# A list scheduler's price for SyncE transfers and its rank for the preparation of later chunk pairs

## The chip, the cores and the metric

One core of one Trainium2 chip. The metric is the device time of one execution in microseconds (us), lowest is best; three runs of the kernel before gave 1113.38, 1113.78 and 1109.34 us, median 1113.38 us.

## The reference

Input: r, k, v, w, a, b of shape (4 batches, 8 heads, 768 steps, 40). Each of the 32 heads runs a linear recurrence over 768 steps with a 40x40 state:

```
y_t   = r_t @ state
Sa    = state @ a_t
state = state * w_t - outer(Sa, b_t) + outer(v_t, k_t)
```

The outputs y of all heads form 3072 tokens of 320 features. They pass a first layer, `max(x@w1, x@w2, x@w3) @ w_out` with 768 hidden units, and a second, `((x@w_a) * (x@w_b)) @ w_out` with 1536 hidden units. All is float32; the matmuls of the two layers are split into a rounded high part and a low part, so that each product takes several matmuls.

## The kernel before, in words

The recurrence is cut into 24 chunks of 32 steps, taken as 12 pairs. `prep(p)` makes what pair p needs and depends on the inputs alone; `chain(c)` carries the state through chunk c; `gather(p)` turns the result of a pair into a 320x256 tile `xf`; `moe_a(p)` is the first layer for that pair's 256 tokens; `moe_b(n)`, n = 0 to 5, is the second layer for 512 tokens each and starts when the recurrence has ended.

**The preparation.** It loads decay and key tiles, runs two scans per chunk on VectorE (L394, L398), and forms products on GpSimd or VectorE and TensorE (L427, L445). A 32x32 triangular system for each head and chunk is then moved through scratch tensors in HBM, since its rows have to change partitions: `BD` is stored at L459 and read back as `BU` at L465; `solve` forms the inverse with alternating multiplies (L499 on GpSimd, L500 on VectorE) and reductions (L501, into `TXp`, then `TW` and `TC`); the inverse is stored to `TD` (L471) and read back as `TT` (L475); the correction block is stored to `ED` (L480) and read back as `NB` (L483).

**The chain.** In each chunk `zmm` (L616) needs the state and the products of the preparation; `half` (L630) needs `TT`; `umm` (L643) needs `NB`; `smm` (L663) gives the new state, which the next chunk's L616 needs. Around them stand transposes (L576, L592, L689) and the output products (L701, L719). `gather` stores at L732 and reads `xf` back at L737 and L739.

**The first layer.** Its weights come in 24 pieces (L759), which VectorE unpacks with four instructions each (L749 to L752); L827 and L852 to L856 are its matmuls, 144 and 48 per pair. `stage_b` unpacks the second layer's weights in 24 more pieces in the same way (load at L916, stores to the scratch tensor `WD` at L923 and L924), and `weights_b` reads them back (L930 to L934) when the recurrence's buffers are free.

**What sets the order.** No order is written by hand. Every operation is recorded with an engine, an estimated duration, a latency after its end, its dependences and a rank `pri`; the function `run` of the class Plan then places one operation after another, each engine taking the ready operation with the earliest start, and among those within 0.05 of it the lowest rank. The latency enters twice: an operation's users count as ready that much later, and the rank is lowered by BL = 0.04 times the length of the longest path behind the operation:

```
            t = d + l + o["pre"]
            bl[i] = t + max((bl[j] for j in out[i]), default=0.0)
            o["pri"] = o["pri"] - BL * bl[i]
```

Ranks that matter here: the chain has 0.001 c (its side products up to 0.5 more), gather 0.2, the first layer's work outside TensorE 0.6 and its matmuls 2 + p, the first layer's weights 3, the second layer's weights 5. The function `dma` records every transfer of SyncE; transfers that ScalarE issues have a function of their own (`adma`) with a latency of 2.0 + bytes/200e3. Where TensorE would idle in the plan, `run` puts matmuls of an identity matrix (L275) into the gap. The program holds the order that results, engine by engine; a transfer that waits holds up all transfers behind it on SyncE's queue.

Of the kernel before, what the change touches and what calls it, by code (L numbers as in the profile page):

```python
# [27 lines left out]
DMIN = 0.4  # L28
# [19 lines left out]
class Plan:  # L48
# [8 lines left out]
    def op(self, eng, dur, fn, r=(), w=(), ps=(), fin=(), pri=0.0, lat=None, after=(), pre=0.0, cls=0, alt=(), act=1.0, bias=None):  # L57

        i = len(self.ops)
        deps = set(after)  # L60
        for k in r:
            if k in self.lw:
                deps.add(self.lw[k])
        for k in w:
            if k in self.lw:
                deps.add(self.lw[k])
            deps.update(self.rd.get(k, ()))
        for k in r:
            self.rd.setdefault(k, []).append(i)
        for k in w:  # L70
            self.lw[k] = i
            self.rd[k] = []
        deps.discard(i)
        ways = {eng: (dur, fn, 0.0)}
        ways.update({e: (d, f, bias if bias is not None else 0.0 if pri < BIASP else BIAS) for e, d, f in alt})
        self.ops.append(dict(i=i, ways=ways, bias=bias, deps=deps, ps=tuple(ps), fin=tuple(fin), pri=pri, lat=lat, pre=pre, cls=cls, act=act))
        return i
# [159 lines left out]
def body(nc, tc, ia, out_ap):  # L237
    from contextlib import ExitStack

    V, A, G, T, SP = nc.vector, nc.scalar, nc.gpsimd, nc.tensor, nc.sync  # L240
    es = ExitStack()
    P = Plan(8)
    op = P.op
    npair = NP

    def dv(n, ps=False):
        return 0.15 + n * 0.00105 if ps else 0.12 + n * 0.0014
# [5 lines left out]
        return 0.4 + n * 0.0023  # L253

    def dma(fn, nbytes, r=(), w=(), pri=0.0, pre=1.2):
        return op("SP", max(DMIN, nbytes / 300e3), fn, r=r, w=w, pri=pri, lat=1.0, pre=pre)

    def adma(fn, nbytes, r=(), w=(), pri=0.0, after=()):

# [70 lines left out]
    def setup():  # L330
        def zero(t, keys, eng, v=0.0, pri=-5.0):
            n = int(np.prod(t.shape[1:]))
            E = {"DVE": V, "POOL": G}[eng]
            op(eng, 0.06 + n * (0.00105 if eng == "DVE" else 0.0009), lambda w_: E.memset(t, v), w=keys, pri=pri)

        R2 = range(2)
        dma(lambda w_: SP.dma_start(con, ia["con"]), 98e3, w=["con"], pri=-9)
        dma(lambda w_: SP.dma_start(TC.rearrange("p i j -> p (i j)")[:, 0:32], ia["one"]), 16e3, w=["TC"], pri=-3)
        zero(d1, ["d1"], "DVE")
        zero(gd, ["gd"], "DVE")  # L340
        zero(RB, [("RB", g) for g in R2], "POOL", pri=-4.5)
        for i, b in enumerate(bank):
            op("ACT", ac(512), lambda w_, b=b: A.activation(b, RB[:, 0].rearrange("p u t -> p (u t)"), AF.Copy), r=[("RB", 0)], w=["bank"], pri=-5.0)
        zero(ZR[0], [(k, 0, g) for k in ("ZRs", "ZRv") for g in R2], "POOL", pri=-4.2)
        zero(YL, [(k, x) for k in ("YLg", "YLr") for x in R2], "POOL", pri=-4)
        zero(YR[0], [(k, 0, x, h) for k in ("YRy", "YRs", "YRs2") for x in R2 for h in R2], "POOL", pri=-4)
        zero(ST, ["ST", ("STx", 0), ("STx", 1)], "POOL", pri=-3)
        for i in range(2):
            op("ACT", ac(512), lambda w_, i=i: A.activation(
                NB[i].rearrange("p c h t -> p (c h) t"), TC.rearrange("p i j -> p (i j)")[:, 0:32].unsqueeze(1).to_broadcast([128, 16, 32]), AF.Copy), r=["TC"], w=[("NB", i, j) for j in range(4)], pri=-3)  # L350
        dma(lambda w_: SP.dma_start(TXp, ia["eye"]), 270e3, w=["TX"], pri=-0.55)


    def prep(p):
        b, kb_ = p % NPB, p % 2
        pr = 1.0 + p - 1.5
        P_, K_, Z_ = Pp[b], KT[kb_], ZL[b]
        parts = [(0, 1), (1, 2)] if p < NSPL else [(0, 2)]

# [23 lines left out]
        for cc in range(2):  # L383
# [8 lines left out]
            else:  # L392
# [8 lines left out]
               r=[("R", cc, 0), ("R", cc, 1), "d1"], w=rc, pri=pr)  # L401
# [4 lines left out]
            for src, k, n in ((Rp[:, cc, :, 0:32], rc, 1), (P_[:, cc, :, 1:33], pc, 0)):  # L406
                op("ACT", 0.61, lambda w_, cc=cc, src=src, n=n: A.activation(
                    Rp[:, cc, :, 0:32], src, AF.Square, accum_out=gd[:, 4 * p + 2 * cc + n:4 * p + 2 * cc + n + 1]),
                   r=k, w=rc + ["gd"], pri=pr + 0.5)
            for g in range(2):  # L410
# [3 lines left out]
                   r=pc, w=[("Za", b, g, cc)], pri=pr, alt=[("DVE", dv(512), lambda w_, cc=cc, g=g, r0=r0: V.tensor_tensor(  # L414
                       Z_[r0:r0 + 64, cc, g], Z_[r0:r0 + 64, cc, g], P_[r0:r0 + 64, cc, :, 0:32], ALU.mult))])
            pn = ("a", "kb", p, cc)
            za = [("Za", b, g, cc) for g in range(2)]
            if p >= KG:
# [12 lines left out]
                for n in range(4):  # L431
# [5 lines left out]
                       r=[pn, "con"], w=[("Zk", b, g, cc)], fin=[pn] if n == 3 else (), pri=pr)  # L437
# [12 lines left out]
            for g in range(2 if p < KG else 0):  # L450
# [4 lines left out]
                   r=[pn, "con"], w=[("Zk", b, g, cc)], fin=[pn] if g else (), pri=pr)  # L455
# [7 lines left out]
        for h in range(2):  # L463
            n, f0 = (512, 0) if h == 0 else (496, 528)
            dma(lambda w_, h=h, n=n, f0=f0: SP.dma_start(  # L465
                BU[64 * h:64 * h + 64].rearrange("p i j -> p (i j)")[:, 0:n],
                BD[b].rearrange("u s t -> u (s t)")[:, f0:f0 + n]), 131e3, r=bk, w=[("BU", h)] + ([("BB", 0)] if h else []), pri=pr)
        solve(p)
        for h in range(2):
            q = 16 * (1 - h)  # L470
# [15 lines left out]
                16e3, r=[("ED", b, h) for h in range(2)], w=[("NB", p % 2, j)], pri=pr)  # L486

    def solve(p):
        pr = 1.0 + p - 1.5
        cnt = [0]  # L490

        def mm(out_v, tmpshape, a, bb, rk, wk):
            i = cnt[0] % 2
            cnt[0] += 1
            n = int(np.prod(tmpshape))
            names = "abcd"[:len(tmpshape)]
            kw = {k: v for k, v in zip(names[1:], tmpshape[1:])}
            tv = TP[i][:, 0:n].rearrange("p (" + " ".join(names) + ") -> p " + " ".join(names), **kw)
            op("POOL", 0.35 + n * 0.0026, lambda w_: G.tensor_tensor(tv, a, bb, ALU.mult), r=rk, w=[("TP", i)], pri=pr,  # L499
               alt=[("DVE", dv(n), lambda w_: V.tensor_tensor(tv, a, bb, ALU.mult))])  # L500
            op("DVE", dv(n, True), lambda w_: V.tensor_reduce(out_v, tv, AX.X, ALU.add), r=[("TP", i)], w=wk, pri=pr)  # L501

        def diag(tile, off, blk, cnt_, rows, cols, rs=32, cs=1):
            base = tile[:, 0:1, 0:1]
            a = base.copy() if False else base
            return bass.AP(tensor=a.tensor, offset=a.offset + off, ap=[list(a.ap[0]), [blk, cnt_], [rs, rows], [cs, cols]])

        bu = [("BU", 0), ("BU", 1)]
        for t in range(1, 8):
            a = diag(TX, 0, 264, 2, t, t)  # L510
            u = diag(BU, t, 264, 2, 1, t, 0, 32)
            u = bass.AP(tensor=u.tensor, offset=u.offset, ap=[list(u.ap[0]), [264, 2], [0, t], [32, t]])
            o = diag(TX, t, 264, 2, t, 1)
            o = bass.AP(tensor=o.tensor, offset=o.offset, ap=[list(o.ap[0]), [264, 2], [32, t]])
            mm(o, (2, t, t), a, u, bu + ["TX"], ["TX"])

        def prod(dst, d_off, d_rs, L, l_off, l_rs, R, r_off, r_rs, nr, nt, nj, rk, wk):
            tl = 512 // (nt * nj)
            for c0 in range(0, nr, tl):
                k = min(tl, nr - c0)  # L520
                lb, rb, db = L[:, 0:1, 0:1], R[:, 0:1, 0:1], dst[:, 0:1, 0:1]
                a = bass.AP(tensor=lb.tensor, offset=lb.offset + l_off + c0 * l_rs, ap=[list(lb.ap[0]), [l_rs, k], [0, nt], [1, nj]])
                u = bass.AP(tensor=rb.tensor, offset=rb.offset + r_off, ap=[list(rb.ap[0]), [0, k], [1, nt], [r_rs, nj]])
                o = bass.AP(tensor=db.tensor, offset=db.offset + d_off + c0 * d_rs, ap=[list(db.ap[0]), [d_rs, k], [1, nt]])
                mm(o, (k, nt, nj), a, u, rk, wk)


        prod(TW, 0, 8, TX, 0, 32, BU, 8, 32, 8, 8, 8, bu + ["TX"], ["TW"])
        prod(TX, 8, 32, TW, 0, 8, TX, 264, 32, 8, 8, 8, ["TX", "TW"], ["TX"])

        op("ACT", 0.3, lambda w_: A.activation(BU[64:128, 0:8, 16:32], BU[0:64, 8:16, 16:32], AF.Copy), r=bu, w=[("BB", 0)], pri=pr)
        for h in range(2):
            op("ACT", 0.35, lambda w_, h=h: A.activation(TU[64 * h:64 * h + 64], TX[64:128, :, 0:16], AF.Copy), r=["TX"], w=[("TU", h)], pri=pr)
        k = bu + [("BB", 0), ("TU", 0), ("TU", 1)]
        prod(TC, 0, 16, BU, 16, 32, TU, 0, 16, 8, 8, 8, k, ["TC"])
        prod(TC, 8, 16, BU, 16, 32, TU, 8, 16, 8, 8, 16, k, ["TC"])
# [477 lines left out]
    stage_b()  # L1014
    ma.extend(range(a0, len(P.ops)))
    prep(0)
    if npair > 1:
        prep(1)
    for p in range(npair):
        a0 = len(P.ops)  # L1020
        chain(2 * p)
        chain(2 * p + 1)
        if p + 2 < npair:
            prep(p + 2)
        gather(p)
        att.extend(range(a0, len(P.ops)))
        a0 = len(P.ops)
        moe_a(p)
        ma.extend(range(a0, len(P.ops)))
# [218 lines left out]
```

## Time and profile before

| | |
|---|---|
| runs | 1113.38 us median of 3 (1109.34 to 1113.78) |
| profiled execution | 1115.33 us, of which the span of instructions is 1113.5 us |
| busy: TensorE, VectorE, ScalarE, GpSimd | 1054.6, 641.5, 481.0, 253.6 us |
| chain that ended last | TensorE 68%, DMA 12%, VectorE 11%, issue 3% |
| moved | 128.99 MB, most of it before 760 us |

The span has two halves that differ. Up to about 713 us the recurrence and the first layer run side by side on all engines; from there the second layer alone keeps TensorE busy. Busy time of TensorE is the union of pipelined matmuls, so it says where nothing at all ran, not how dense the rest was.

### The profile page before, as it was taken

How to read it: one execution, taken by the hardware profiler on the slowest of the kernel's cores; microseconds unless marked ns; L12 is line 12 of the kernel's file. 1: busy time of each engine (PE TensorE's matmuls, PEld its weight loads, DVE VectorE, ACT ScalarE, POOL GpSimd, SP SyncE). 2: the span in 40 equal slices, each digit the busy share in tenths (PEclk: the TensorE clock that was granted, in tenths of full speed). 3: DMA queues.
4: the chain of work that ended last, by engine and by line, in shares of the span. 5: the costliest groups of instructions: out<-in, count | busy, mean ns of one | idle time of the engine just before them, and what ended most of it. 6: DMA issues, size and time to landing. Idle time of an engine off the chain costs nothing.

```text
span 1113.5 us, 34271 instructions
## 1 busy us (share of the span) xinstructions
PE 1054.6 (95%) x14826; PEld 949.6 (85%) x14826; DVE 641.5 (58%) x1052; ACT 481.0 (43%) x1112; POOL 253.6 (23%) x219
## 2 busy tenths in 40 slices
PE   8899898989799999989999999999999999999997
PEld 7777798889798888888888889988888888888886
DVE  6778598768797966887787744333223232322222
ACT  5246364737465554647363662222223222322221
POOL 3343264324244542424242310000000000000000
PEclk8989798989899988999999999999999999999999
DMA  8746764666567657585846556870101000000000
GB/s 254 178 93 170 176 158 100 148 155 175 134 189 164 173 139 175 131 195 140 202 104 158 148 154 186 250 174 11 43 1 53 1 24 1 1 24 1 24 1 26
DMA packets 177661, 128.99 MB, mean 116 GB/s; under 512 B 122848, under 2 KB 150624, under 8 KB 176544
## 3 DMA queue, kind: packets, MB, share of 16 engines
q1 hardware_dynamic: 174048, 120.84, 42.8%
q10 hardware_dynamic: 3456, 5.90, 1.5%
q8 instruction: 118, 1.93, 0.7%
q14 instruction: 39, 0.32, 0.1%
HBM read 96.02 MB, written 30.67 MB: 114 GB/s over the span
## 4 chain that ended last, share of the span: by engine, by line
PE 68%; DMA 12%; DVE 11%; issue 3%; SPq 2%; ACT 2%; POOL 1%; ACTq 0%; DVEq 0%; POOLq 0%
PE bank L967 24%; PE bank L827 11%; PE bank L975 4%; PE bank L977 4%; PE bank L976 4%; DMA wraw<-in_wpa_dram 2%; DMA WD<-wraw 2%; PE bank L719 2%; PE bank L663 2%; PE bank L275 2%; PE bank L701 2%; PE bank L630 2%; PE bank L576 1%; DMA ED<-TC 1%; PE bank L852 1%
## 5 line engine op out<-in xcount | busy, mean ns | idle before, releaser
L985 DVE TENSOR_TENSOR bas<-bank,bas 128x512 f32<-128x512 f32 x72 | 49.8, 692 | 213.5 <-PE bank L967 207.1
L967 PE MATMUL bank<-bxhi,bw 128*128 128x512 f32 x576 | 156.3, 393 | 0.0
L967 PEld LDWEIGHTS bank<-bxhi,bw 128*128 128x128 f32 x576 | 106.1, 188 | 20.8
L987 ACT ACTIVATE bgh<-bas 128x512 fp32r<-128x512 f32 x72 | 45.6, 633 | 143.9 <-DVE bas L985 142.0
L984 ACT ACTIVATE bas<-bank 128x512 f32<-128x512 f32 x72 | 43.0, 598 | 137.3 <-PE bank L967 137.3
L827 PE MATMUL bank<-xhi,whi 128*128 128x256 f32 x432 | 99.0, 312 | 0.0
L827 PE MATMUL bank<-xhi,wlo 128*128 128x256 f32 x432 | 91.3, 295 | 0.0
L827 PE MATMUL bank<-xlo,whi 128*128 128x256 f32 x432 | 90.9, 294 | 0.0
L967 PE MATMUL bank<-bxlo,bw 128*128 128x512 f32 x288 | 89.7, 393 | 0.0
L975 PE MATMUL bank<-bo,bgh 128*128 128x320 f32 x288 | 88.9, 309 | 0.0
L977 PE MATMUL bank<-bo,bgl 128*128 128x320 f32 x288 | 88.8, 308 | 0.0
L976 PE MATMUL bank<-bo,bgh 128*128 128x320 f32 x288 | 88.8, 308 | 0.0
L988 DVE TENSOR_TENSOR bgl<-bas,bgh 128x512 fp32r<-128x512 f32 x72 | 49.8, 692 | 47.0 <-ACT bgh L987 46.9
L842 DVE TENSOR_TENSOR hm<-bank,hm 128x512 f32<-128x512 f32 x72 | 49.6, 689 | 46.8 <-PE bank L827 45.6
L827 PEld LDWEIGHTS bank<-xhi,whi 128*128 128x128 f32 x432 | 70.7, 203 | 2.9
L827 PEld LDWEIGHTS bank<-xhi,wlo 128*128 128x128 f32 x432 | 71.8, 204 | 0.1
L827 PEld LDWEIGHTS bank<-xlo,whi 128*128 128x128 f32 x432 | 71.4, 203 | 0.0
L499 POOL TENSOR_TENSOR TP<-TXp,BU 128x50 f32<-128x50 f32 (+7 forms) x67 | 47.5, 709 | 101.6 <-DVE TXp L501 56.5
L412 POOL TENSOR_TENSOR ZL<-ZL,Pp 64x512 f32<-64x512 f32 x37 | 54.9, 1484 | 57.3 <-DVE Pp L394 29.7
L275 PE MATMUL bank<-con 128*128 128x128 f32 x452 | 62.7, 297 | 2.8 <-DMA con<-in_con_dram 2.8
L967 PEld LDWEIGHTS bank<-bxlo,bw 128*128 128x128 f32 x288 | 54.1, 188 | 12.3
L827 PE MATMUL bank<-xl,wt 128*128 128x256 f32 x216 | 63.3, 293 | 0.5 <-POOL xl L819 0.5
(161 smaller groups left out, 2496.8 us busy)
## 6 DMA issues: line engine op xcount, KB each, us to landing
wraw<-in_wpb_dram SPq DMA_DIRECT2D x24, 480.0 KB
KT<-in_kb_dram SPq DMA_DIRECT2D x20, 384.0 KB
bw<-WD SPq DMA_DIRECT2D x12, 512.0 KB
WD<-wraw ACTq DMA_DIRECT2D x24, 240.0 KB
WD<-wca SPq DMA_DIRECT2D x24, 240.0 KB
Pp<-in_wf_dram SPq DMA_DIRECT2D x10, 528.0 KB
Rp<-in_wr_dram SPq DMA_DIRECT2D x10, 528.0 KB
wraw<-in_wpa_dram SPq DMA_DIRECT2D x12, 384.0 KB
```

Source lines behind the costliest of these rows:

```text
L275: P.keep = lambda b: T.matmul(bank[b][:, 0:128], ident, ident, start=True, stop=True)
L412: op("POOL", po(512), lambda w_, cc=cc, g=g, r0=r0: G.tensor_tensor(Z_[r0:r0 + 64, cc, g], Z_[r0:r0 + 64, cc, g], P_[r0:r0 + 64, cc, :, 0: ...
L499: op("POOL", 0.35 + n * 0.0026, lambda w_: G.tensor_tensor(tv, a, bb, ALU.mult), r=rk, w=[("TP", i)], pri=pr, alt=[("DVE", dv(n), lambda w ...
L827: T.matmul(ps, w, x, start=(i == 0), stop=(i == 7))
L842: op("DVE", dv(512, True), lambda w_, pn=pn: V.tensor_tensor(f(hm), bank[w_[pn]], f(hm), ALU.max), r=[pn], w=["hm"], fin=[pn], pri=ep)
L967: T.matmul(ps, w, x, start=(k == 0), stop=(k == 7))
L975: T.matmul(o, gh[:, c], oh, start=ff == 0, stop=False)
L976: T.matmul(o, gh[:, c], ol, start=False, stop=False)
L977: T.matmul(o, gl[:, c], oh, start=False, stop=ff == 11)
L985: op("DVE", dv(512, True), lambda w_, j=j, pb=pb: V.tensor_tensor(tb["as", j], bank[w_[pb]], tb["as", j], ALU.mult), r=[pb], w=[("bas", j) ...
L987: op("ACT", ac(512), lambda w_, j=j, k=k: A.activation(tb["gh", k], tb["as", j], AF.Copy), r=[("bas", j)], w=[("gh", k)], pri=ep)
L988: op("DVE", dv(512), lambda w_, j=j, k=k: V.tensor_tensor(tb["gl", k], tb["as", j], tb["gh", k], ALU.subtract), r=[("bas", j), ("gh", k)], ...
```

## The change

The latency that the scheduler books for a SyncE transfer was 1.0 us for any size and becomes 2.0 us plus bytes/200e3, the same form as for ScalarE's transfers (for 131,000 bytes 2.66 instead of 1.0). The rank of `prep(p)` and `solve(p)` was p - 0.5 and becomes 0.6 p - 0.5: pair 0 stays at -0.5, pair 2 goes from 1.5 to 0.7, pair 6 from 5.5 to 3.1, pair 11 from 10.5 to 6.1. No operation of the computation is added or removed.

```
--- before.py
+++ after.py
@@ -253,7 +253,7 @@
         return 0.4 + n * 0.0023
 
     def dma(fn, nbytes, r=(), w=(), pri=0.0, pre=1.2):
-        return op("SP", max(DMIN, nbytes / 300e3), fn, r=r, w=w, pri=pri, lat=1.0, pre=pre)
+        return op("SP", max(DMIN, nbytes / 300e3), fn, r=r, w=w, pri=pri, lat=2.0 + nbytes / 200e3, pre=pre)
 
     def adma(fn, nbytes, r=(), w=(), pri=0.0, after=()):
 
@@ -353,7 +353,7 @@
 
     def prep(p):
         b, kb_ = p % NPB, p % 2
-        pr = 1.0 + p - 1.5
+        pr = -0.5 + 0.6 * p
         P_, K_, Z_ = Pp[b], KT[kb_], ZL[b]
         parts = [(0, 1), (1, 2)] if p < NSPL else [(0, 2)]
 
@@ -486,7 +486,7 @@
                 16e3, r=[("ED", b, h) for h in range(2)], w=[("NB", p % 2, j)], pri=pr)
 
     def solve(p):
-        pr = 1.0 + p - 1.5
+        pr = -0.5 + 0.6 * p
         cnt = [0]
 
         def mm(out_v, tmpshape, a, bb, rk, wk):
```

The order that comes out differs on every engine. Three places follow.

SyncE, around the tables of pair 4, before the change. `XD`, `xf` belong to the gather of pair 3; `TD`, `TT`, `ED`, `NB` to the tables of pair 4; `BD`, `BU` to pair 5:

```order
L732 DMA XD_81<-XY 40x4x256 x2
L374 DMA Pp_120<-in_wf_dram 128x1056
L862 DMA X2D_84<-x2s 128x512
L737 DMA xf<-XD_81 128x2x256
L739 DMA xf<-XD_81 64x256 x2
L863 DMA X2D_84<-x2s 64x256
L916 DMA wraw<-in_wpb_dram 128x960
L471 DMA TD_75<-TXp 64x512 x2
L459 DMA BD_73<-ZL_128 32x16x32 x4
L374 DMA Rp<-in_wr_dram 128x1056
L480 DMA ED_78<-TC 64x128 x2
L475 DMA TT_140<-TD_75 32x16x32 x4
```

and the stretch that holds the same tables of pair 4 after the change:

```order
L471 DMA TD_75<-TXp 64x512 x2
L556 DMA XX<-in_vx_dram 32x640
L924 DMA WD<-wca 128x480
L916 DMA wraw<-in_wpb_dram 128x960
L556 DMA XX<-in_vx_dram 32x640
L475 DMA TT_140<-TD_75 32x16x32
L567 DMA YL<-in_ry_dram 40x512 x2
L475 DMA TT_140<-TD_75 32x16x32 x3
L556 DMA ZR_136<-in_vz_dram 32x640 x2
L480 DMA ED_78<-TC 64x128 x2
L459 DMA BD_73<-ZL_128 32x16x32 x2
L563 DMA XT<-in_vt_dram 80x16x32
```

The tables' stores no longer stand behind the read-back of the gather (L737, L739); they now come before that gather's own store. Other transfers stand between L471 and L475 in both.

TensorE, up to the `half` (L630) of the first chunk of pair 4, before:

```order
L856 MATMUL bank_65<-hlo,woh 128x256
L827 MATMUL bank_67<-xhi,whi 128x256 x2
L827 MATMUL bank_67<-xhi,wlo 128x256 x2
L827 MATMUL bank_67<-xlo,whi 128x256 x2
L827 MATMUL bank_67<-xt_109,wt_103 128x256
L827 MATMUL bank_67<-xl_110,wt_103 128x256
L827 MATMUL bank_66<-xhi,whi 128x256 x2
L827 MATMUL bank_66<-xhi,wlo 128x256 x2
L827 MATMUL bank_66<-xlo,whi 128x256 x2
L827 MATMUL bank_66<-xt_109,wt_103 128x256
L827 MATMUL bank_66<-xl_110,wt_103 128x256
L630 MATMUL bank_64<-Zs,TT_140 32x40 x32
```

and after:

```order
L827 MATMUL bank_68<-xhi,wlo 128x256 x2
L827 MATMUL bank_68<-xlo,whi 128x256 x2
L827 MATMUL bank_68<-xt_109,wt_103 128x256
L827 MATMUL bank_68<-xl_110,wt_103 128x256
L701 MATMUL bank_69<-RB,XT 64x64 x16
L576 MATMUL bank_65<-con,KT_124 128x104 x4
L827 MATMUL bank_64<-xhi,whi 128x256 x2
L827 MATMUL bank_64<-xhi,wlo 128x256 x2
L827 MATMUL bank_64<-xlo,whi 128x256 x2
L827 MATMUL bank_64<-xt_109,wt_103 128x256
L827 MATMUL bank_64<-xl_110,wt_103 128x256
L630 MATMUL bank_70<-Zs,TT_140 32x40 x32
```

Before the change 99 rows stand between this chunk's L616 and its L630, with 112 matmuls of L827 and 24 of L852 to L856; after it 13 rows with 16 matmuls of L827.

SyncE near the end of the recurrence, after the change (`bw`, `bt`, `bo` are the second layer's weights, read back; `wraw` is the load of a piece of them that is still to be unpacked):

```order
L932 DMA bt_10352<-WD 64x2x128 x2
L934 DMA bo_10353<-WD 128x2x320
L862 DMA X2D_94<-x2s 128x512
L863 DMA X2D_94<-x2s 64x256
L932 DMA bt_10352<-WD 64x2x128 x2
L934 DMA bo_10353<-WD 128x2x320 x2
L941 DMA xr_10354<-X2D_87 128x8x64
L916 DMA wraw<-in_wpb_dram 128x960
L924 DMA WD<-wca 128x480
L944 DMA xr_10354<-X2D_87 64x4x64 x2
L941 DMA xr_10354<-X2D_88 128x8x64
L924 DMA WD<-wca 128x480
```

Before the change the 24th and last load of L916 stands ahead of all reads of `bw`; now it stands behind the reads of the first nine parts.

Over the whole program the identity matmuls of L275 rise from 226 to 256 instructions (the trace shows two records for each).

## Rows read from the trace of the kernel before

**Rows 1.** Busy time by stretch: length, PE, PEld, DVE, ACT, POOL, granted clock, DMA.

```profile
0.00:150.00 150.00, 135.33 (x2289) 114.78 (x2290) 109.09 (x194) 72.00 (x190) 55.87 (x54) 0.87 0.67 168
150.00:650.00 500.00, 462.13 (x9643) 429.57 (x9645) 388.60 (x638) 284.06 (x704) 192.75 (x161) 0.94 0.62 156
650.00:713.00 63.00, 62.78 (x875) 60.57 (x870) 28.53 (x49) 21.22 (x47) 4.96 (x4) 1.00 0.71 210
713.00:1113.50 400.50, 394.31 (x2033) 344.63 (x2031) 115.32 (x173) 103.69 (x174) 0.00 (x0) 1.00 0.11 31
```

**Rows 2.** Timeline of TensorE: L616 of chunks 6, 7 and 8.

```profile
208.15 0.80 PE L616 MATMUL bank<-ZR,ZL 128*32 128x40 f32 x64
...
247.54 0.80 PE L616 MATMUL bank<-ZR,ZL 128*32 128x40 f32 x64
...
261.08 0.71 PE L616 MATMUL bank<-ZR,ZL 128*32 128x40 f32 x55
```

**Rows 3.** Waits of TensorE: us in total, times, longest.

```profile
PE bank L630 <- DMA TT<-TD: 19.9, 15, 3.1
...
PE bank L643 <- DMA NB<-ED: 3.5, 6, 1.2
```

**Rows 4.** Timeline of TensorE, L630 of chunk 8; in brackets the idle time before it.

```profile
284.51 0.97 PE L630 MATMUL bank<-Zs,TT 32*32 32x40 f32 x6 [1.90 <-DMA TT<-TD]
```

**Rows 5.** Timeline of VectorE, the last reduction into pair 4's inverse.

```profile
267.50 0.69 DVE L501 TENSOR_REDUCE TXp<-TP 128x64 f32<-128x512 f32 x1
```

**Rows 6.** Timeline of SyncE's queue around the tables of pair 4.

```profile
267.68 1.18 SPq L862 DMA_DIRECT2D X2D<-x2s  x1
272.05 0.37 SPq L737 DMA_DIRECT2D xf<-XD  x1
272.51 1.13 SPq L739 DMA_DIRECT2D xf<-XD  x2
...
274.95 2.27 SPq L471 DMA_DIRECT2D TD<-TXp  x2
...
281.45 4.66 SPq L475 DMA_DIRECT2D TT<-TD  x4
```

**Rows 7.** Waits of SyncE's queue for a store to land before its read-back.

```profile
SPq L483 <- DMA ED<-TC: 13.3, 6, 4.1
...
SPq L737 <- DMA XD<-XY: 8.0, 7, 2.6
...
SPq L475 <- DMA TD<-TXp: 7.1, 3, 2.9
...
SPq L465 <- DMA BD<-ZL: 5.4, 4, 1.6
```

**Rows 8.** Groups by line: busy us, mean ns of one, idle before.

```profile
L275 PE MATMUL bank<-con 128*128 128x128 f32 x452 | 62.7, 297 | 2.8 <-DMA con<-in_con_dram 2.8
...
L752 DVE SCALAR_TENSOR_TENSOR wraw<-wraw,wca 128x480 f32<-128x480 uint32 (+3 forms) x48 | 32.5, 677 | 0.4
L750 DVE SCALAR_TENSOR_TENSOR wraw<-wraw,wca 128x480 uint32<-128x480 uint32 (+3 forms) x48 | 30.6, 637 | 0.4
...
L749 DVE TENSOR_SCALAR wca<-wraw 128x480 uint32<-128x480 uint32 (+3 forms) x48 | 26.2, 546 | 44.7 <-DMA wraw<-in_wpa_dram 23.6 <-DMA wraw<-in_wpb_dram 10.4 <-DMA WD<-wca 6.1
...
L751 DVE TENSOR_SCALAR wca<-wraw 128x480 uint32<-128x480 uint32 (+3 forms) x48 | 22.4, 466 | 0.3
```

**Rows 9.** Chain that ended last: start us, us, what; a block of 16 first-layer matmuls.

```profile
660.78 2.10 PE bank L827 x16
```

**Rows 10.** Timeline of SyncE's queue: the last piece of weights, loaded and stored.

```profile
662.67 0.39 SPq L916 DMA_DIRECT2D wraw<-in_wpb_dram  x1
...
679.58 0.54 SPq L924 DMA_DIRECT2D WD<-wca  x1
...
721.73 0.78 SPq L930 DMA_DIRECT2D bw<-WD  x1
...
732.09 0.60 SPq L934 DMA_DIRECT2D bo<-WD  x1
```

More of the change, by code (lines that the diff above doesn't have):

```diff
@@ L255, in dma @@
     def dma(fn, nbytes, r=(), w=(), pri=0.0, pre=1.2):
-        return op("SP", max(DMIN, nbytes / 300e3), fn, r=r, w=w, pri=pri, lat=1.0, pre=pre)
+        return op("SP", max(DMIN, nbytes / 300e3), fn, r=r, w=w, pri=pri, lat=2.0 + nbytes / 200e3, pre=pre)
     def adma(fn, nbytes, r=(), w=(), pri=0.0, after=()):
@@ L355, in prep @@
         b, kb_ = p % NPB, p % 2
-        pr = 1.0 + p - 1.5
+        pr = -0.5 + 0.6 * p
         P_, K_, Z_ = Pp[b], KT[kb_], ZL[b]
@@ L488, in solve @@
     def solve(p):
-        pr = 1.0 + p - 1.5
+        pr = -0.5 + 0.6 * p
         cnt = [0]
```

## The prediction

> **What bounds the kernel now.** I read the busy time by stretch first [rows 1]. [...]
>
> [...] The state products (L616) of chunks 6, 7 and 8 begin at 208.2, 247.5 and 261.1 us [rows 2]: from the first chunk of a pair to its second 39 us pass, from the second to the next pair only 14. The two chunks do the same work, so the first one waits for something: the waits of TensorE name it [rows 3], the tables TT (19.9 us in 15 waits) and NB (3.5 us in 6), together 23.4 us. For pair 4 the trace shows the whole way. The last reduction into the inverse ends at 268.2 us [rows 5], but its store to TD starts only at 274.95 and the read-backs into TT only at 281.45 [rows 6]; L630 then starts at 284.5 after an idle 1.9 us [rows 4]. Ahead of the store SyncE's queue held the gather's read-back (L737, L739), which waited for its own store to land. Such waits, a store just ahead of its read-back, cost that queue 13.3 + 8.0 + 7.1 + 5.4 = 33.8 us [rows 7]. A plan that books 1.0 us for each of these transfers puts the read-back too close behind the store, and everything behind it stands.
>
> **The change, part by part.**
>
> *Room between stores and read-backs.* I counted, in the two orders, the transfers that stand on SyncE between the last store and the first read-back, over all 12 pairs: for BD and BU 30 before and 83 after, for XD and xf 40 and 70, for ED and NB 41 and 61, for TD and TT 51 and 55. In all 162 become 269. The 33.8 us of queue time should shrink. On TensorE this is worth at most the 23.4 us of [rows 3], and nothing at least, if the tables are late for another reason (the solve itself). I take half, -12 us: three of the four gaps grow by half or more, but the one that ends in TT, which is the larger wait, hardly grows, and its gain has to come from the places where the store itself stands earlier, as in pair 4.
>
> *Preparation ahead of the first layer's weights.* Ahead of the last reduction for pair 2 stand 231 VectorE instructions before and 200 after; the largest part is six weight pieces less, counted at L749, and five less at L750 to L752. By [rows 8] that is 6 x 0.55 + 5 x (0.64 + 0.47 + 0.68) = 12 us of VectorE time in front of pair 2's tables. What is gained there is lent: when pair 2's L630 comes up in TensorE's order, 16 matmuls of L827 are behind it instead of 80. A block of 16 takes 2.10 us [rows 9], 0.131 each, so 64 matmuls are 8.4 us that have to be done later on an engine that is 92% busy. The identity matmuls ahead of that L630 also fall, from 205 to 194. Between a gain of 12 and a loss of 8.4 I take 0.
>
> *Identity matmuls.* 30 more instructions are 60 more records; one record costs 62.7/452 = 0.139 us [rows 8], so 8.3 us if all of them take time from real work and 0 if all stand in real gaps. 13 of the 30 stand behind the last L616, where TensorE is busy for 62.8 of 63 us today [rows 1]; the others fall mostly where TensorE waits anyway. I take 13 x 2 x 0.139 = +3.6 us.
>
> *The last piece of second-layer weights* now loads behind the reads of nine finished parts. Today the last piece takes 17 us from its load at 662.7 to its last store at 679.6, and the read of the remaining three parts runs from 721.7 to 732.1 [rows 10], 10 us. So 27 us after the second layer's start the three parts can be there; 72 blocks in 400.5 us [rows 1] are 5.6 us each, so the tenth block, the first to need them, comes after 50 us. I cost it at 0; the cover is nine blocks that have their weights. If it went, the rest of those 27 us would show as a hole around 760 us; I leave 5 us for it in the range.
>
> Sum against the profiled execution, 1115.3 us: -12 + 0 + 3.6 + 0 = -8.4, so 1106.9. That execution lies 1.95 us above the median of the runs, and the same -8.4 from 1113.4 gives **1105.0 us**.
>
> **The rivals.** About 0.5%, 5.6 us here, is what a measurement of this kernel can tell from no change.
>
> *Full order (no change).* TensorE is 92% busy between 150 and 650 us, and both orders hold the same real work. If the waits of [rows 3] only change place, because what comes early in one pair is paid for in the next, the time stays at 1113, within 5.6. For it: everything lent in the early stage comes back before the last chunk (1440 matmuls of L827 stand ahead of the last L616 in both orders). Against it: a wait for the queue's head is work for nobody, and its cause is reduced.
>
> *The preparation sets the pace.* If VectorE's order decides when a pair starts, both gains arrive in full: 12 us early and 23.4 in the waits, less the 8.3 of identity matmuls, -27 and so 1086. For it: 39 against 14 us in [rows 2]. Against it: TensorE has too little idle time to give so much.
>
> *Halves without cover (slower).* Between L616 and L630 of the first chunk, the new order has little for TensorE to do in three pairs: 16 first-layer matmuls instead of 136 in pair 4, 24 instead of 96 in pair 6, 8 instead of 80 in pair 7. The plan trusts that the tables are there by then. If they come no earlier than today, the lost cover is 264 matmuls, 264 x 0.131 = 35 us of standing still; it decides as soon as TT lands later than that little work ends, in pair 4 some 2 us of first-layer matmuls and a few transposes after L616. Part of it would be caught up, as the deferred matmuls fill later gaps: those are 38 us wide in all, of which some 15 could take it. So +35 - 15 + 3.6 = +24, 1137. For it: in pair 4 three of the four read-backs of TT now stand behind a transfer (L567) that must wait for a product of the chain. Against it: the store of TD comes before the gather there.
>
> [...]
>
> That the change does not do what it says is excluded: the orders differ on every engine as shown.
>
> **How the numbers follow.** The forecast, -5.6 to -20 us, has a chance of 0.40, the preparation's pace 0.13; together faster 0.53. The full order has 0.25. Halves without cover has 0.17 and the clock 0.05, together slower 0.22. The forecast's own range, from the bounds of its costs, is 1093 to 1108. The range for 8 in 10 reaches down into the second faster case and up over the clock's case: 1090 to 1126; below it lies most of the preparation's case (0.09), above it most of the halves without cover (0.11).
>
> **What would show it.** Right: TensorE's waits for TT and NB fall from 23.4 us to about 12; SyncE's four waits fall from 33.8 us to under 20; L616 of the last chunk comes about 10 us earlier than now; the second layer still takes 400 us. The preparation's pace would show as a pair period clearly under 53 us. Wrong: waits of L630 longer than 4 us each in pairs 4, 6 and 7; a granted clock under 0.9 between 450 and 550 us; or a hole in the second layer near its tenth block. If TT and NB waits vanish and the time stays, the order was full and I was wrong about what idle time is worth.

## The result, and the profile after

| | before | after | ratio after/before, 95% interval |
|---|---|---|---|
| first comparison | 1113.45 us (4 runs) | 1099.75 us (4 runs, 1097.52 to 1103.52) | 0.9889 [0.9852, 0.9925] |
| second comparison | 1112.71 us | 1104.7 us (6 runs, 1094.85 to 1110.3) | 0.9892 [0.9837, 0.9946] |

The ratios leave out runs more than 1.5% above the fastest of their kernel, and they are not the quotients of the medians shown, which are over all runs.

The changed kernel is 1.1% faster, about 12 us. The forecast was 1105.0 us in a range of 1090 to 1126: the sign and the range hold; the median of the first comparison lies 5 us below the forecast, that of the second within half a microsecond of it. The profiled execution took 1097.52 us, with a span of 1095.5.

Busy time by stretch of the kernel after (length, PE, PEld, DVE, ACT, POOL, granted clock, DMA); the third stretch ends where the second layer begins, as in [rows 1]:

```profile
0.00:150.00 150.00, 136.59 (x2633) 118.83 (x2633) 122.01 (x207) 81.42 (x214) 58.73 (x54) 0.98 0.76 187
150.00:650.00 500.00, 459.28 (x9828) 427.11 (x9830) 393.37 (x648) 283.76 (x702) 194.57 (x157) 0.95 0.62 154
650.00:696.40 46.40, 46.40 (x419) 46.19 (x414) 19.56 (x32) 11.75 (x21) 1.97 (x2) 1.00 0.75 223
696.40:1095.50 399.10, 392.65 (x2019) 343.11 (x2017) 117.26 (x177) 102.63 (x172) 1.24 (x1) 1.00 0.12 34
```

The second layer takes 399.1 us against 400.5, so nearly the whole difference lies ahead of it, 16.5 of the 18.0 us between the two spans: it begins at 696.4 instead of 712.9. The long stretch in the middle is as full as it was (459 us busy, before 462). In the first 150 us TensorE runs 344 matmul records more than before, VectorE is busy for 122.0 instead of 109.1 us, and the granted clock is 0.98 instead of 0.87.

The waits that the forecast was built on, TensorE's of the kernel after (engine and line, what it waited for: us in total, times, longest); these answer to [rows 3]:

```profile
PE bank L701 <- ACT XT L692: 6.9, 2, 6.6
PE bank L630 <- issue: 4.7, 2, 2.6
PE bank L576 <- DVE XY L723: 4.7, 2, 4.2
PE bank L592 <- DVE ST L675: 4.4, 2, 3.5
...
PE bank L643 <- DMA NB<-ED: 2.9, 4, 2.1
...
PE bank L630 <- DMA TT<-TD: 1.6, 1, 1.6
```

TT and NB together are down from 23.4 to 4.5 us. But the first four lines were absent or shorter before, and TensorE's whole idle time ahead of the second layer is not smaller: 712.9 - 660.1 = 52.8 us before, 696.4 - 642.3 = 54.1 after (the busy time before from a view further down, after from the first three rows above). SyncE's queue kept less of the waits of [rows 7]:

```profile
SPq L737 <- DMA XD<-XY: 5.7, 5, 2.6
SPq L475 <- DMA TD<-TXp: 4.9, 3, 3.0
SPq L465 <- DMA BD<-ZL: 4.2, 4, 2.0
...
SPq L483 <- DMA ED<-TC: 1.9, 3, 0.9
```

That is 16.7 us instead of 33.8. For pair 4, the forecast's example, the way can be followed again, against [rows 4 to 6]. First VectorE's last reduction into the inverse (start, us):

```profile
233.84 0.69 DVE L501 TENSOR_REDUCE TXp<-TP 128x64 f32<-128x512 f32 x1
```

Then SyncE's queue:

```profile
234.55 1.14 SPq L471 DMA_DIRECT2D TD<-TXp  x2
...
239.01 0.37 SPq L475 DMA_DIRECT2D TT<-TD  x1
239.69 0.66 SPq L567 DMA_DIRECT2D YL<-in_ry_dram  x2
240.41 2.48 SPq L475 DMA_DIRECT2D TT<-TD  x3
```

And TensorE, chunk 8:

```profile
241.49 0.80 PE L616 MATMUL bank<-ZR,ZL 128*32 128x40 f32 x64
...
246.69 0.79 PE L630 MATMUL bank<-Zs,TT 32*32 32x40 f32 x64
```

The store follows the reduction at once (before: 6.8 us later), four other transfers fill the time until the first read-back, and the last read-back is issued by 242.9, ahead of L630. L630 has no idle time in brackets now. From the end of the reduction to L630 it is 12.2 us instead of 16.3, and from L616 to L630 5.2 instead of 23.4, with only 16 matmuls of L827 between them. So little work was enough cover.

**Where the 16.5 us of the profiled pair come from.** Four marks of the same program divide the first part: L616 of chunks 4, 10 and 22, and the first L967, which begins the second layer. Kernel before, TensorE's timeline:

```profile
150.79 0.84 PE L616 MATMUL bank<-ZR,ZL 128*32 128x40 f32 x64
...
314.51 0.80 PE L616 MATMUL bank<-ZR,ZL 128*32 128x40 f32 x64
...
636.39 0.80 PE L616 MATMUL bank<-ZR,ZL 128*32 128x40 f32 x64
```

Kernel after, the same chunks, and the first L967:

```profile
130.07 0.36 PE L616 MATMUL bank<-ZR,ZL 128*32 128x40 f32 x10
...
276.68 0.80 PE L616 MATMUL bank<-ZR,ZL 128*32 128x40 f32 x64
...
606.69 0.80 PE L616 MATMUL bank<-ZR,ZL 128*32 128x40 f32 x64
...
696.45 0.48 PE L967 MATMUL bank<-bxhi,bw 128*128 128x512 f32 x1
```

The recurrence is 20.7 us ahead at chunk 4 and 37.8 at chunk 10; then it gives back 8.1 until chunk 22 and 13.2 more until the second layer. What it gives back is seen in the first-layer matmuls of these stretches (L827 alone: us, busy, records, granted clock, DMA). Before:

```profile
0.00:150.80 150.80, 3.63 (x24) 0.88 0.67 168
150.80:314.50 163.70, 59.99 (x408) 0.93 0.61 152
314.50:636.40 321.90, 139.02 (x968) 0.95 0.63 159
636.40:712.90 76.50, 43.14 (x328) 1.00 0.68 197
```

After:

```profile
0.00:130.10 130.10, 0.00 (x0) 0.97 0.75 184
130.10:276.70 146.60, 47.63 (x328) 0.94 0.64 157
276.70:606.70 330.00, 137.52 (x1000) 0.95 0.63 158
606.70:696.40 89.70, 52.11 (x400) 1.00 0.64 183
```

Up to chunk 10, 328 of the 1728 matmuls are done instead of 432; up to chunk 22, 1328 instead of 1400. The 72 that are left for the end are 72 x 0.131 = 9.4 us of the last stretch's 13.2; beside them this stretch holds 32 more matmuls of L852 to L856 and 31 more records of L275.

### The profile page after: what moved, and what is told of

It reads as the page before. It is cut to its first block, busy times and chain, and to the rows that moved or that the text cites. A ratio compares the mean times of both kernels' runs of the same rounds, so it can differ in the third digit from the quotient of the medians.

```text
span 1095.5 us, 34391 instructions
## 1 busy us (share of the span) xinstructions
PE 1034.9 (94%) x14886; PEld 935.2 (85%) x14886; DVE 652.2 (60%) x1062; ACT 479.6 (44%) x1108; POOL 256.5 (23%) x213
## 4 chain that ended last, share of the span: by engine, by line
PE 71%; DVE 11%; DMA 8%; issue 4%; ACT 3%; SPq 2%; POOL 1%; ACTq 0%; DVEq 0%; POOLq 0%
PE bank L967 24%; PE bank L827 12%; PE bank L977 4%; PE bank L975 4%; PE bank L976 4%; PE bank L275 3%; PE bank L701 2%; PE bank L719 2%; PE bank L663 2%; DMA WD<-wraw 1%; PE bank L852 1%; PE bank L576 1%; PE bank L592 1%; PE bank L643 1%; PE bank L616 1%
## 5 line engine op out<-in xcount | busy, mean ns | idle before, releaser
L967 PE MATMUL bank<-bxhi,bw 128*128 128x512 f32 x576 | 156.4, 393 | 0.0
L967 PEld LDWEIGHTS bank<-bxhi,bw 128*128 128x128 f32 x576 | 106.2, 188 | 20.8
L827 PE MATMUL bank<-xhi,whi 128*128 128x256 f32 x432 | 96.6, 306 | 0.2 <-DVE ZL L433 0.2
L967 PE MATMUL bank<-bxlo,bw 128*128 128x512 f32 x288 | 89.8, 393 | 0.0
L827 PE MATMUL bank<-xhi,wlo 128*128 128x256 f32 x432 | 88.6, 287 | 0.0
L827 PE MATMUL bank<-xlo,whi 128*128 128x256 f32 x432 | 88.5, 287 | 0.0
L412 POOL TENSOR_TENSOR ZL<-ZL,Pp 64x512 f32<-64x512 f32 x42 | 58.6, 1396 | 76.0 <-DVE Pp L394 41.9
L275 PE MATMUL bank<-con 128*128 128x128 f32 x512 | 69.9, 290 | 4.3 <-DMA con<-in_con_dram 2.8
L827 PEld LDWEIGHTS bank<-xhi,whi 128*128 128x128 f32 x432 | 68.2, 196 | 3.5 <-DVE ZL L433 0.4
L827 PEld LDWEIGHTS bank<-xhi,wlo 128*128 128x128 f32 x432 | 69.0, 196 | 0.0
L275 PEld LDWEIGHTS bank<-con 128*128 128x128 f32 x512 | 64.2, 201 | 5.6 <-ACT bank L343 2.8
L827 PEld LDWEIGHTS bank<-xlo,whi 128*128 128x128 f32 x432 | 68.7, 196 | 0.0
L499 POOL TENSOR_TENSOR TP<-TXp,BU 128x2 f32<-128x2 f32 (+7 forms) x56 | 38.6, 688 | 112.3 <-DVE TXp L501 69.9
L967 PEld LDWEIGHTS bank<-bxlo,bw 128*128 128x128 f32 x288 | 54.1, 188 | 12.2
```

The costliest lines, as they stand in the source:

```text
L275: P.keep = lambda b: T.matmul(bank[b][:, 0:128], ident, ident, start=True, stop=True)
L412: op("POOL", po(512), lambda w_, cc=cc, g=g, r0=r0: G.tensor_tensor(Z_[r0:r0 + 64, cc, g], Z_[r0:r0 + 64, cc, g], P_[r0:r0 + 64, cc, :, 0: ...
L827: T.matmul(ps, w, x, start=(i == 0), stop=(i == 7))
L967: T.matmul(ps, w, x, start=(k == 0), stop=(k == 7))
```

## The experiments

Two theories stood at first. **Order**: the gain comes from where the plan puts the transfers (WAITS in the expectations) and the preparation (EARLY PREPARATION). **Clock**: it comes from the 30 further identity matmuls of L275, through the clock that is granted to TensorE, in the first 150 us 0.87 before and 0.98 after. The second was tempting: in the profiled pair TensorE's idle time is the same within 1.3 us, and the difference is busy time, 660.1 us at a granted 0.93 against 642.3 at 0.96. The low-clock time of the expectations is the time at a granted clock of 0.50: cut into windows of 1 us, the first 175 us of the kernel before show 1.00 in 134 windows, 0.50 in 32 and a value between in 9, which makes 38 us at 0.50; those of the kernel after show 160, 9 and 6, 10 us. Ahead of the second layer it is 96 us before and 55 after. Each kernel was timed beside the kernel before; ratios are to that.

**Each half of the change alone.** Latency only, the kernel before with

```
-        return op("SP", ..., pri=pri, lat=1.0, pre=pre)
+        return op("SP", ..., pri=pri, lat=2.0 + nbytes / 200e3, pre=pre)
```

> The new latency alone, ranks as before. Its order holds 42 and 101 identity matmuls ahead of the first and between the first and second L616 (30 and 82 before the change, 47 and 95 after it). Theory CLOCK (the gain is low-clock time of TensorE in the first 175 us, 38 us before and 10 after, removed by identity matmuls that fill the gaps): low-clock time there under 15 us and most of the gain, 1098 to 1105. Theory WAITS (the gain is the waits for TT and NB, 23.4 us before and 4.5 after, which only the latency moves): waits under 8 us and the whole gain, 1098 to 1102. Theory EARLY PREPARATION (the gain is pair 1 and pair 2 being prepared ahead of the first layer's weights, which only the rank does): 1110 to 1116.

Rank only, the kernel before with, in `prep` and in `solve`,

```
-        pr = 1.0 + p - 1.5
+        pr = -0.5 + 0.6 * p
```

> The new rank alone, latency 1.0 as before; 41 and 60 identity matmuls in the two early stretches, 11 fewer than before the change. CLOCK: low-clock time in the first 175 us stays at 30 us or more, 1110 to 1118. WAITS: waits for TT and NB stay at 20 us or more, 1110 to 1116. EARLY PREPARATION: the fifth L616 comes about 20 us earlier, as after the change (130 instead of 151 us), and the time is 1098 to 1104.

Latency only: 1102.9 us, 0.9923 [0.9887, 0.9959], by the ratio 8.6 us faster. Rank only: 1120.5 us, 1.0057 [1.0024, 1.0089], slower, and above all three ranges that were set for it. TensorE's waits with the latency only:

```profile
PE bank L643 <- DMA NB<-ED: 5.8, 4, 2.7
PE bank L630 <- DMA TT<-TD: 5.5, 11, 1.1
```

and with the rank only:

```profile
PE bank L630 <- DMA TT<-TD: 14.5, 14, 3.2
PE bank L643 <- DMA NB<-ED: 8.2, 8, 3.2
```

The latency alone halves the two waits, 23.4 to 11.3 us; the rank alone leaves them at 22.7. SyncE's four waits of [rows 7] go the same way: 19.3 us with the latency alone and 41.3 with the rank alone, where the kernel before has 33.8. Busy time ahead of the second layer, before:

```profile
0.00:712.90 712.90, 660.14 (x12795) 604.83 (x12796) 526.22 (x879) 377.24 (x938) 253.59 (x219) 0.93 0.64 163
```

latency only:

```profile
0.00:702.40 702.40, 657.55 (x12942) 606.63 (x12942) 527.20 (x890) 376.20 (x937) 244.15 (x204) 0.96 0.65 163
```

Idle time falls from 52.8 to 44.9 us, so of the 12 us that left the two waits 8 left the stretch. What the rank alone does shows in its L827 by stretch, up to the L616 of chunk 22 and from there to the second layer:

```profile
0.00:609.20 609.20, 167.64 (x1168) 0.90 0.66 161
609.20:719.80 110.60, 72.57 (x560) 1.00 0.63 179
```

Its recurrence is far ahead as well (chunk 22 at 609 instead of 636 us), but 560 matmuls instead of 328 are left for the end, 232 x 0.131 = 30 us, and that is more than the lead. Which part of the 6 us it loses comes from this debt and which from SyncE's longer waits was not tried apart.

**The new rank in some pairs only**, both with the new latency. In the early pairs:

```
-        pr = -0.5 + 0.6 * p
+        pr = -0.5 + (0.6 * p if p < 4 else p)
```

> New latency, new rank in pairs 0 to 3 alone, old rank from pair 4 on. If the part of the gain that the clock does not explain (7 to 8 us at equal clock) lies in the early stage: 1098 to 1103, as the whole change, and the fifth L616 near 130 us. If it lies in the later pairs: 1103 to 1108, as the latency alone.

and in the later ones:

```
-        pr = -0.5 + 0.6 * p
+        pr = -0.5 + (p if p < 4 else 0.6 * p)
```

> New latency, old rank in pairs 0 to 3, new rank from pair 4 on. If the part that the clock does not explain lies in the early stage: 1102 to 1108, as the latency alone. If it lies in the later pairs: 1096 to 1102.

The changed kernel itself ran beside them:

> The changed kernel once more, beside the next three. All theories: 1098 to 1103, ratio to before 0.985 to 0.992; mean granted clock 0.965 to 0.973.

Early pairs: 1103.4 us, 0.9893 [0.9844, 0.9942]; the changed kernel 1104.7, 0.9892; late pairs 1112.4, 1.0000 [0.9965, 1.0034]. In time, the new rank from pair 4 on adds nothing that can be told. But the kernel with the early pairs alone has a cost of its own that hides what the later pairs do. In its profiled execution the second layer begins at 694.7 us, as early as that of the changed kernel, and then takes 408.0 us instead of 399.1. A piece of the second layer's weights comes late, and TensorE stands:

```profile
749.82 2.08 PE L967 MATMUL bank<-bxhi,bw 128*128 128x512 f32 x4 [6.27 <-DMA bw<-WD]
```

So this pair of kernels does not settle what the rank is worth from pair 4 on.

The last kernel, at 1112.4 us above both ranges that were set for it, undoes what the latency gives, but it is not a clean half of the change: its rank drops from 2.5 in pair 3 to 1.9 in pair 4, so pair 4 ranks ahead of pair 3. Its recurrence stands for long between L616 and L630 of pairs 3, 6 and 9; for chunk 12, the first of pair 6, TensorE's timeline has

```profile
354.64 0.26 PE L616 MATMUL bank<-ZR,ZL 128*32 128x40 f32 x5
...
401.32 0.79 PE L630 MATMUL bank<-Zs,TT 32*32 32x40 f32 x64
```

46.7 us from one to the other, where the kernel before takes 17.4 and the changed one 6.0. TensorE does other work in most of that time, but its idle time ahead of the second layer is 712.5 - 652.9 = 59.6 us, the most of the kernels that keep the identity matmuls and have the new latency.

**The identity matmuls.** Four kernels test the clock theory. The changed order without 28 of the first 142:

```
-    P.keep = lambda b: T.matmul(...)
+    P.keep = lambda b, n=[0]: n.__setitem__(0, n[0] + 1) or [T.matmul(...) for _ in range(int(n[0] > 142 or n[0] % 5 > 0))]
```

> The changed kernel, the same order of all else, without every fifth of the first 142 identity matmuls (28 fewer; 114 left ahead of the second L616, 112 before the change). CLOCK: low-clock time in the first 175 us rises from 10 to 25 us or more and the time to 1106 to 1112. WAITS and EARLY PREPARATION: the order does it, so 1097 to 1101, the low-clock time may rise but the fifth L616 stays near 130 us.

The old order with 28 of the first 112 doubled:

```
-    P.keep = lambda b: T.matmul(...)
+    P.keep = lambda b, n=[0]: n.__setitem__(0, n[0] + 1) or [T.matmul(...) for _ in range(1 + int(n[0] <= 112 and n[0] % 4 == 0))]
```

> The kernel before, the same order of all else, with every fourth of the first 112 identity matmuls doubled (28 more). CLOCK: low-clock time in the first 175 us falls from 38 to under 20 us and the time to 1100 to 1107. WAITS and EARLY PREPARATION: no gain, 1112 to 1118, since the added matmuls may also take time.

And each order, as planned, with none of them:

```
-    P.keep = lambda b: T.matmul(...)
+    P.keep = lambda b: None
```

> The changed kernel without any identity matmul of L275, all else in the same order (256 instructions left out; they feed no result). CLOCK: low-clock time before the second layer at least doubles from 55 us and the time rises to 1120 to 1145, by about 0.4 us for each us of low-clock time. ORDER (the gain lies in what the engines do, the clock is a by-product): the 70 us of identity matmuls stood in gaps, the time stays within 1095 to 1110.

The 0.4 us in it for each us of low-clock time is the author's estimate; the profiled pair gives the same, 16.5 us over 96 - 55 = 41.

> The kernel before without any identity matmul of L275, all else in its order (226 instructions left out; they feed no result). ORDER (the change gains by the order of the real work, the identity matmuls matter little either way): within 1105 to 1116, that is 8 to 18 us above the changed kernel without them (1097.7). CLOCK, in the weaker form that is left (the old order needs the added identity matmuls, the new one does not): 1118 or more. FILLS COST (identity matmuls only cost time in both orders): 1100 to 1106.

The changed order: 1102.9 us without the 28, 0.9926 [0.9893, 0.9958], and 1097.7 with none, 0.9853 [0.9800, 0.9907], the lowest median of all kernels here. The old order: 1107.7 with 28 more, 0.9955 [0.9926, 0.9985], and 1108.4 with none, 0.9963 [0.9930, 0.9996]. The old order without them:

```profile
0.00:704.20 704.20, 614.46 (x12342) 555.36 (x12343) 532.27 (x879) 377.39 (x938) 257.91 (x219) 0.90 0.66 165
```

and the changed order without them:

```profile
0.00:694.00 694.00, 615.25 (x12359) 553.77 (x12360) 532.64 (x885) 376.32 (x935) 256.55 (x212) 0.90 0.66 166
```

The granted clock falls from 0.93 and 0.96 to 0.90 in both, and neither kernel is slower without them, 1108.4 us beside 1111.9 and 1097.7 beside 1104.7. With the same clock the changed order still begins the second layer 10.2 us earlier. So the clock theory fell: the order is worth its 1% with or without identity matmuls. That a few more of them and none at all both take less than 0.5% off the old order is not explained.

Two more of this kind, the changed order with the first 142 left out (`n[0] <= 142 or T.matmul(...)`),

> The changed kernel without its first 142 identity matmuls (all those ahead of the second L616), the other 114 kept, all else in the same order. ORDER: 1095 to 1103, between the changed kernel and the one without any. [...]

and the changed kernel planned anew with `P.keep = None`, so that the plan itself holds no identity matmuls:

> The changed scheduler with its identity matmuls switched off in the plan too, so that the order is made anew (256 instructions left out, and real work moves). ORDER: what counts is how much first-layer work is left behind the last chunks: its order holds 1216 matmuls of L827 ahead of the L616 of chunk 22 instead of 1328, 112 more after it, 15 us at 0.131 each; 1100 to 1112. FILLS COST: 1092 to 1099, as without them in the old plan or better.

The first took 1104.0 us, 0.9924 [0.9891, 0.9957], no different from the changed kernel. The second took 1120.5, 1.0087 [1.0054, 1.0119], above both ranges that were set for it: without the matmuls the planner finds another order, which leaves 512 matmuls of L827 behind the L616 of chunk 22, as the rank alone leaves 560.

**The latency alone, without identity matmuls.** What remained open was whether the latency alone accounts for the gain also where the clock is the same in all kernels.

> The kernel with the new latency alone, in the order that was planned for it, with none of the identity matmuls of L275 issued; no result depends on them. Without identity matmuls the old order took 1108.4 us and the changed order 1097.7, so 10.7 us lie between the two orders where the granted clock has no fills to thank for. If the room between stores and read-backs carries the gain and the new rank adds nothing, this kernel comes out with the changed order: 1095 to 1101 us, with the waits of L630 and L643 for DMA under 15 us (26.8 in the old order without fills). If the rank in the early pairs is what carries it, this kernel stays near the old order: 1104 to 1110 us. If each carries a part, about 1102. The spread between single runs of such a kernel is some 10 us, so a result between 1101 and 1104 leaves it open.

It took 1099.1 us, 0.9908 [0.9872, 0.9944]. Its first part:

```profile
0.00:697.00 697.00, 615.39 (x12358) 554.08 (x12358) 523.90 (x889) 375.88 (x937) 249.81 (x204) 0.91 0.66 164
```

The waits of the old order without identity matmuls:

```profile
PE bank L630 <- DMA TT<-TD: 14.9, 15, 3.2
...
PE bank L643 <- DMA NB<-ED: 11.9, 6, 7.4
```

and with the new latency:

```profile
PE bank L630 <- DMA TT<-TD: 7.4, 11, 2.0
...
PE bank L643 <- DMA NB<-ED: 2.5, 2, 1.3
```

Here time and idle time agree. TensorE's busy time is the same in the three kernels (614.5, 615.4 and 615.3 us for the old order, the latency alone and both parts), so all that moves is idle time: 89.7, 81.6 and 78.8 us. The latency brings 8.1 us of that and the rank 2.9 more; in time 1108.4, 1099.1 and 1097.7 us. These three medians come from three sessions. Against the kernel before in the same session they are 0.9963, 0.9908 and 0.9853, and by this the latency brings only half of the 1.1%. So the latency's part is shown, half of the gain by one reckoning and most of it by the others. The rank's part on top of it stays open, since the intervals of the last two ratios overlap. Open too is the way in which the latency works: it makes users ready later, and it lowers ranks through the path lengths, and no run took the two apart.

## Why the prediction was right, step by step

**Room between stores and read-backs (-12): right in kind and nearly in size.** Alone, the latency takes 12.1 us from the waits for TT and NB, brings 7.9 us less idle time and 8.6 us (interval 4.6 to 12.6) in time. So "I take half" met what the latency alone does to the waits, but the text let every microsecond of wait count as time, and a third of the 12.1 comes back as other idle time. In the whole change the two waits fall further, to 4.5 us, and TensorE's idle time in the profiled pair does not fall with them: L701, L576 and L592 wait instead, for ScalarE and VectorE.

**Preparation ahead of the weights (0): the number was met, the gain behind it was not.** It set a gain of at most 12 us against a debt of 8.4. The debt was well counted: at pair 2's L630 the trace has 16 matmuls of L827 behind it instead of 80, and at chunk 22 72 are still owed, 9.4 us. The gain was not: L616 of chunk 4 comes 20.7 us earlier and that of chunk 10 37.8. And it was put to the wrong part of the change. With the rank alone chunk 22 is 27 us ahead and the kernel is slower. With the latency alone it is 25 us ahead (611.8 us) and the kernel is faster, though 14 of the 25 us are given back before the second layer; it leaves 344 matmuls of L827 for the end and not 560. So the latency moves the preparation forward as well. The code offers a reason, which was not tried apart: a longer booked delay lengthens every path through the preparation, and the planner orders by such paths (the term `BL * bl[i]`). What the rank adds to the latency cannot be told from 0, so the term's 0 stands, but by luck: the gain was sized too small, and the latency, which the text gave no part in it, brings it too.

**Identity matmuls (+3.6): too high.** L275 rose as counted, to 512 records:

```profile
L275 PE MATMUL bank<-con 128*128 128x128 f32 x512 | 69.9, 290 | 4.3 <-DMA con<-in_con_dram 2.8 <-issue 1.5
```

Its busy time is 7.2 us more, near the upper bound of 8.3. But busy is not cost: leaving out all 226 in the old order gave 3.5 us (1111.9 to 1108.4), which would make 30 of them 0.5 us; leaving out all 256 in the changed order gave 7.0 (1104.7 to 1097.7), which would make it 0.8. The 13 behind the last L616 were not tried apart.

**The last piece of weights (0): right.** Kernel after, SyncE's queue:

```profile
700.38 0.52 SPq L916 DMA_DIRECT2D wraw<-in_wpb_dram  x1
...
716.22 0.32 SPq L924 DMA_DIRECT2D WD<-wca  x1
...
727.75 0.60 SPq L934 DMA_DIRECT2D bo<-WD  x1
```

The last read is issued 31 us after the second layer's start, the forecast said 27, and the tenth block is 50 us away. The second layer has no hole and takes 399.1 us. That such a cover can fail is shown by the kernel with the new rank in the early pairs alone, whose hole of 6.3 us ends at 749.8.

**The sum (-8.4).** It lies in the intervals of both ratios, at the edge of the first (-8.3 to -16.5 us of 1113.4) and well inside the second (-6.0 to -18.1 of 1112.7). It is nearer than its terms: the latency alone is worth -8.6 and not -12, the identity matmuls some +0.5 to +0.8 and not +3.6. These two misses cancel, and that is luck.

**The signs.** TensorE's waits for TT and NB fell to 4.5 us and not to about 12, which is where the latency alone leaves them; SyncE's four waits fell to 16.7, under 20 as said. L616 of the last chunk comes at 636.4 us instead of 655.4, 19 us earlier and not 10 (649.7 in a second profiled execution). None of the signs of being wrong came.

**The rivals.** *Full order* described half of what happened: waits change place, and idle time in the profiled pair did not fall. But the text's own sentence, that waits which vanish at an unchanged time would show a full order, has its answer in the time, which fell. *The preparation sets the pace* did not come: from chunk 4 to 22 a pair takes 53.0 us (before 54.0). *Halves without cover*, whose 38 us of gaps are the 500 us of the long stretch less the 462.13 busy in [rows 1], did not come in the changed kernel, where L616 and L630 of pairs 4, 6 and 7 lie 5.2, 6.0 and 3.3 us apart and L630 does not wait; the tables are there. *The clock* (a chance of 0.05, and a part of the range up to 1126): no run shows the term behind them. Between 450 and 550 us, where the text looked for its sign, 0.98 is granted and before 0.97. Without identity matmuls the granted clock up to the second layer falls further, from 0.96 to 0.90 in the changed order, and the time does not rise with it: 1097.7 us is the lowest median here. In one place matmuls take longer: behind the hole of 6.3 us in the kernel with the new rank in the early pairs alone, four matmuls of L967 take 2.08 us, where four like them took 1.09 at 732.6 us in the changed kernel; of the group they belong to, the longest took 796 ns, the median 394. The clock that was granted just there was not read.

## What to carry to other kernels

A planner that books too short a delay for a transfer can make an order in which a queue stands, with transfers behind the waiting one that could go: with 1.0 us booked, SyncE's longest waits for a store were 1.6 to 4.1 us [rows 7], and pair 4's store to TD was issued 6.8 us after its data was there [rows 5 and 6]. Booking a longer delay gained here by itself, and re-ranking by itself lost; whether 2.0 us plus bytes/200e3 is the best size was not tried. A rank that pulls one stage forward must be read by what it leaves for the end. Count the work that stands behind the last step of the chain before believing a lead in the middle. When a wait disappears, look at the engine's whole idle time before booking the gain, and compare it over several kernels: one profiled pair put the whole gain into busy time, and kernels at the same granted clock put it into idle time.

## What the runs showed that was not expected

The same kernel can take its time differently from one execution to the next. In the profiled execution of the second comparison the changed kernel began its second layer at 709.7 us and not at 696.4, with 53.4 us idle in place of 54.1:

```profile
0.00:709.70 709.70, 656.28 (x12869) 603.24 (x12870) 532.62 (x885) 376.94 (x936) 252.63 (x212) 0.94 0.65 163
```

The busy time is 14.0 us longer (656.3 against 642.3), at a granted clock of 0.94 instead of 0.96: in these two executions of one kernel, clock and time go together. Among twenty executions of the kernel before in one session, the fastest, 1106.0 us, had a mean granted clock of 0.969 and the slowest, 1121.0, of 0.953. From one kernel to another they did not here: the changed order without identity matmuls has a granted clock of 0.90 up to the second layer and a profiled span of 1092.8 us, with them 0.96 and 1095.5. The clock it loses lies above all at the start, where

```profile
0.00:150.00 150.00, 115.11 (x2161) 86.80 (x2162) 117.33 (x200) 78.82 (x206) 59.15 (x53) 0.74 0.73 177
```

stands against the 136.59 us busy at 0.98 of the changed kernel's first row. In the traces of the kernels before and after, 166 and 169 of the first 175 windows of 1 us have a granted clock of either 1.00 or 0.50. If this stretch is mixed of the same two values, 0.74 puts about half of it at 0.50, 0.26/0.50 by estimate. TensorE is idle for 34.9 us of it all the same: its speed is not what this stretch lacks.
